# Two attention blocks side by side: first weight rows for six heads in one load, second x pair in two, first products at full width

## The chip, the cores and the metric

The kernel runs on one core of a Trainium2 chip. The metric is the time of one execution in microseconds of device time. A run also has a span, from the first to the last instruction of the core; here the time is about 1.8 us longer than the span. The profile lists instructions by engine: PE (matrix products; PEld are its weight loads, which overlap the products: 213.6 us of them beside 335.2 us of products in a span of 341.2 us), DVE (vector), ACT (scalar), POOL, and SP, which here issues most DMA loads.

## The reference

Two independent blocks, A and B, do the same work on different data, and their outputs stand side by side in the last dimension. Cut to what matters:

```python
# x [16, 32, 1024], k_cache/v_cache [16, 4, 512, 128], wq [1024, 4096], wo [4096, 1024], bf16
def block(x, k_cache, v_cache, wq, wo):
    q = (x @ wq).reshape(16, 32, 32, 128).transpose(0, 2, 1, 3)
    k, v = (jnp.repeat(t, 8, axis=1) for t in (k_cache, v_cache))   # 8 query heads per KV head
    p = softmax(einsum("bhqd,bhkd->bhqk", q, k) * 128 ** -0.5)
    o = einsum("bhqk,bhkd->bhqd", p, v)
    return o.transpose(0, 2, 1, 3).reshape(16, 32, 4096) @ wo
# result: concatenate([block(A), block(B)], axis=-1)
```

The change touches only the first microseconds of block A: `x @ wq` for the first eight heads.

## The kernel before

x has 512 tokens (TT = 4 tiles of 128) and 1024 columns (DC = 8 chunks of 128). The product for one head and one chunk takes 128 rows of wq as weights and 128 rows of x transposed (xT) as the moving operand, 512 tokens wide. The first four chunks of x are loaded plainly and transposed by PE into PSUM; DVE copies chunks 0 and 2 into SBUF, ACT chunks 1 and 3. The first eight heads are computed chunk by chunk as data arrives (NF = 6 heads first, then the other two). The loads, in order of issue:

```python
load_x(0, TT // 2, TT, nc.scalar)        # x chunks 0-1, second token half, issued by ACT
load_x(0, 0, TT // 2)                    # x chunks 0-1, first token half; this and the rest by SP
load_w0(0, 1, 0, NF // 2)                # wq chunk 0, heads 0-2  (96 KB)
load_w0(0, 1, NF // 2, NF)               # wq chunk 0, heads 3-5  (96 KB)
load_w0(1, 2, 0, NF)                     # wq chunk 1, heads 0-5  (192 KB)
load_x(2, 0, TT)                         # x chunks 2-3           (256 KB)
load_w0(2, 3, 0, NF)                     # wq chunk 2
load_w0(3, 4, 0, NF)                     # wq chunk 3
# ... (heads 6-7, chunks 4-7, the k and v caches)
```

The work of PE at the start, where `transpose_x` is four or two PE transposes and a copy, and `first_heads(heads, chunks, t0, t1)` is one product per head and chunk over the given token tiles:

```python
warm_up(22)                                              # dummy products of 128 columns
for k, ts in enumerate(((0, TT // 2), (TT // 2, TT))):   # token halves
    transpose_x(0, *ts, nc.vector.tensor_copy)
    transpose_x(1, *ts, nc.scalar.copy, spare[k])
for ts in ((0, TT // 2), (TT // 2, TT)):
    first_heads(range(0, NF // 2), (0,), *ts)            # 3 heads, half width, twice
first_heads(range(NF // 2, NF), (0,))                    # 3 heads, full width
first_heads(range(0, NF - 2), (1,))
transpose_x(2, 0, TT, nc.vector.tensor_copy)
transpose_x(3, 0, TT, nc.scalar.copy)
# ... the rest of the first eight heads, then a stream of products for the other heads (L301),
#     scores (L357), values (L425) and the output projection (L320), to the end
```

## Time and profile before

| | before |
|---|---|
| time, median of 3 runs (range) | 343.14 us (342.83 to 343.26) |
| span of the profiled run | 341.2 us |
| PE busy | 335.2 us, 98% |
| first product of chunk 0 starts | 4.17 us |
| first product of the stream (second group of heads) starts | 18.91 us |

The profile's page gives busy time by engine, and the chain of work that ended last, followed back from the last instruction:

```profile
PE 335.2 (98%) x2082; PEld 213.6 (63%) x2121; DVE 265.5 (78%) x336; ACT 185.9 (54%) x209; POOL 46.7 (14%) x206
...
PE 98%; issue 1%; ACT 0%; ACTq 0%
```

PE alone bounds the kernel. The timeline of the start of before follows. Its columns: start in us, length in us, engine, line, operation, output and input, shapes, and how many instructions are merged in the row; in brackets the idle time of the engine before it and what ended it. A merged row names only the first shape: the 13 products of the row at 4.17 are six of half width (256 columns) and seven of full width.

```profile
2.92 0.53 PE L516 MATMUL q_ps<-const-bfloat16-1.0 128*128 128x128 bf16 x3
3.28 1.09 PE L524 MATMUL xT_ps<-ident,x_sb 128*128 128x128 bf16 x8
3.71 0.29 DVE L528 COPY xT<-xT_ps 128x256 bf16<-128x256 bf16 x1 [2.75 <-PE xT_ps L524]
3.92 0.86 ACT L528 COPY xT<-xT_ps 128x256 bf16<-128x256 bf16 x2 [1.32 <-PE xT_ps L524]
4.17 2.79 PE L534 MATMUL q_ps<-xT,w_sb 128*128 128x256 bf16 x13
4.19 0.29 DVE L528 COPY xT<-xT_ps 128x256 bf16<-128x256 bf16 x1 [0.19 <-PE xT_ps L524]
5.79 0.67 PEld L534 LDWEIGHTS <-w_sb 128*128 128x128 bf16 x4 [0.20 <-DMA w_sb<-in_A_wq_dram]
6.79 0.61 PE L524 MATMUL xT_ps<-ident,x_sb 128*128 128x128 bf16 x8
7.45 0.83 PE L534 MATMUL q_ps<-xT,w_sb 128*128 128x512 bf16 x3
```

The products of chunk 0 start at 4.17 us, before DVE has even begun its second copy (4.19 us): the half-width products of the first token half hide that copy. The one weight load that waited (0.20 us at 5.79) cost nothing, because a product was still running (starts at 5.71 and 5.93 us, 0.216 us apart like those after them).

One thing this view doesn't show directly. The start times of single products in the trace tell how fast PE runs: until 5.10 us products of 256 columns start 213 ns apart, after it 110 ns. The array's clock doubles there. Transposes of 128 columns agree: those before 4.17 us start 107 ns apart except around their waits, like the warm-up products, and those from 6.79 us on 56 ns.

### The profile page before, as it was taken

The numbers are of one execution on the slowest core, as the hardware profiler recorded it, in microseconds if no ns is written. First come the engines' busy times: TensorE is split into PE (matmuls) and PEld (weight loads), VectorE is DVE, ScalarE is ACT, GpSimd is POOL, SyncE is SP. The second block draws the span as 40 slices with busy tenths as digits, with TensorE's granted clock in tenths as the row PEclk, the third lists the DMA queues.
The fourth block names the chain that finished last, engine by engine and source line by source line (L and its number), as shares of the span: only waits on it lengthen the run. The fifth ranks groups of instructions, "written<-read, shape, count | busy, mean of one in ns | idle before, by whom it ended". The sixth has DMA issues, their size and how long they took to land.

```text
span 341.2 us, 5454 instructions
## 1 busy us (share of the span) xinstructions
PE 335.2 (98%) x2082; PEld 213.6 (63%) x2121; DVE 265.5 (78%) x336; ACT 185.9 (54%) x209; POOL 46.7 (14%) x206
## 2 busy tenths in 40 slices
PE   8999999999999999999999999999999999999996
PEld 6455666666666666666666666666666666666555
DVE  1046988888988898888888988879888888889540
ACT  3058666666667667666645545555555555555110
POOL 0001110011111111110012221222122101111100
PEclk9999999999999999999999999999999999999999
DMA  7999999999996987899999955998449997430001
GB/s 211 287 190 273 285 249 202 233 242 268 291 248 154 232 242 219 210 314 299 308 306 258 250 125 144 334 268 242 118 103 296 356 187 176 104 97 16 18 18 33
DMA packets 128094, 71.70 MB, mean 210 GB/s; under 512 B 75840, under 2 KB 127296, under 8 KB 128064
## 3 DMA queue, kind: packets, MB, share of 16 engines
q1 hardware_dynamic: 127264, 70.07, 84.1%
q0 software_dynamic: 384, 1.05, 0.9%
q8 instruction: 17, 0.28, 0.3%
q10 hardware_dynamic: 416, 0.20, 0.2%
q14 instruction: 13, 0.11, 0.1%
HBM read 50.86 MB, written 2.10 MB: 155 GB/s over the span
## 4 chain that ended last, share of the span: by engine, by line
PE 98%; issue 1%; ACT 0%; ACTq 0%
PE f_ps L320 32%; PE q_ps L301 28%; PE ob L425 17%; PE s_ps L357 16%; PE q_ps L534 4%; PE q_ps L516 1%; PE xT_ps L524 0%; ACT o_sb L329 0%; ACTq L329 0%
## 5 line engine op out<-in xcount | busy, mean ns | idle before, releaser
L365 ACT ACTIVATE p_sb<-s_ps,shift 128x1024 bf16<-128x1024 f32 x128 | 142.7, 1115 | 97.5 <-PE s_ps L357 88.1
L376 DVE TRANSPOSE_TENSOR_REDUCE parts<-p_sb 128x32 f32<-128x1024 bf16 x128 | 158.7, 1240 | 21.0 <-ACT p_sb L365 19.3
L320 PE MATMUL f_ps<-wo_sb,oT 128*128 128x512 bf16 (+1 forms) x525 | 128.2, 366 | 0.6
L301 PE MATMUL q_ps<-xT,wq_sb 128*128 128x512 bf16 x430 | 113.2, 379 | 0.5
L425 PE MATMUL ob<-p_sb,v_sb 128*128 128x256 bf16 x512 | 76.8, 273 | 0.8
L357 PE MATMUL s_ps<-qT,kT 128*128 128x256 bf16 x512 | 76.8, 273 | 0.0
L320 PEld LDWEIGHTS <-oT 128*128 128x128 bf16 x544 | 53.2, 98 | 35.3
L357 PEld LDWEIGHTS <-kT 128*128 128x128 bf16 x512 | 56.9, 113 | 28.3
L301 PEld LDWEIGHTS <-wq_sb 128*128 128x128 bf16 x448 | 43.8, 98 | 32.2
L425 PEld LDWEIGHTS <-v_sb 128*128 128x128 bf16 x512 | 50.1, 98 | 20.0
L447 DVE TENSOR_TENSOR oT<-r,ob 128x512 bf16<-128x512 f32 x64 | 43.9, 686 | 19.9 <-PE ob L425 19.4
L411 DVE STREAM_TRANSPOSE r<-rall 128x512 f32<-128x512 f32 x64 | 44.2, 691 | 1.1
L309 ACT CAST qT<-q_ps 128x512 bf16<-128x512 f32 x56 | 32.7, 583 | 16.5 <-PE q_ps L301 16.5
L394 POOL COPY half<-cs 64x32 f32<-64x32 f32 x32 | 6.5, 204 | 231.8 <-DVE cs L384 231.8
L329 ACT CAST o_sb<-f_ps 128x512 bf16<-128x512 f32 (+1 forms) x17 | 9.5, 559 | 23.6 <-PE f_ps L320 23.6
L534 PE MATMUL q_ps<-xT,w_sb 128*128 128x512 bf16 (+1 forms) x65 | 14.4, 379 | 0.1
L384 DVE TENSOR_REDUCE cs<-parts 128x32 f32<-128x128 f32 x32 | 12.1, 377 | 1.1
L406 DVE RECIPROCAL rall<-sums 128x32 f32<-128x32 f32 x32 | 10.2, 319 | 3.3 <-POOL sums L403 3.3
L534 PEld LDWEIGHTS <-w_sb 128*128 128x128 bf16 x67 | 6.8, 102 | 7.0 <-DMA w_sb<-in_A_wq_dram 0.2
L560 DVE CAST qT<-q_ps 128x512 bf16<-128x512 f32 x4 | 2.5, 684 | 10.2 <-PE q_ps L534 10.2
L331 POOL DMA_DIRECT2D out_dram<-o_sb x8 | 4.6, 574 | 29.3 <-ACT o_sb L329 29.3
L395 POOL TENSOR_TENSOR half<-half,cs 64x32 f32<-64x32 f32 x32 | 7.8, 243 | 2.6
(25 smaller groups left out, 44.7 us busy)
## 6 DMA issues: line engine op xcount, KB each, us to landing
v_sb<-in_A_v_cache_dram SPq DMA_DIRECT2D x16, 512.0 KB, 5.7
wq_sb<-in_B_wq_dram SPq DMA_DIRECT2D x8, 1024.0 KB, 5.7
wo_sb<-in_A_wo_dram SPq DMA_DIRECT2D x8, 1024.0 KB, 7.4
v_sb<-in_B_v_cache_dram SPq DMA_DIRECT2D x16, 512.0 KB, 4.7
wo_sb<-in_B_wo_dram SPq DMA_DIRECT2D x8, 1024.0 KB, 8.1
wq_sb<-in_A_wq_dram SPq DMA_DIRECT2D x5, 1024.0 KB, 5.8
wq_sb<-in_A_wq_dram SPq DMA_DIRECT2D x2, 512.0 KB, 6.7
kT<-in_A_k_cache_dram SPq DMA_TRANSPOSE x64, 4.4
```

What stands on the lines that cost most here:

```text
L301: nc.tensor.matmul(ps[:], lhsT=w[:, dc, (h % 4) * DH:(h % 4 + 1) * DH], rhs=xT[pr][:, dc, :], start=(dc == 0), stop=(dc == DC - 1),)
L309: nc.scalar.copy(out=qT[pr, g][:, :, hl, :], in_=ps[:].rearrange("p (b s) -> p b s", s=SQ),)
L320: nc.tensor.matmul(ps[:, 0:width], lhsT=oT[pr, tt][:, h, :], rhs=wo_tiles[pr, nh, h // REP][:, h % REP, off:off + width], start=(h == 0), ...
L357: nc.tensor.matmul(s_ps[:, c, :], lhsT=kT[:, i % GRP, c, :], rhs=qT[pr, g][:, b, :, :].rearrange("p h s -> p (h s)"), start=True, stop=True,)
L365: nc.scalar.activation(out=p_sb[:], in_=s_ps[:], func=ACTF.Exp, bias=shift[:], scale=SCALE)
L376: nc.vector.tensor_reduce(out=parts[k][:, q, :, :].rearrange("p c h -> p (c h)"), in_=st[i]["p"][:].rearrange("p c (h s) -> p (c h) s", s=SQ),
L384: nc.vector.tensor_reduce(out=cs[:], in_=parts.pop(k)[:].rearrange("p q c h -> p q h c"), axis=AX.X, op=ALU.add,)
L406: nc.vector.reciprocal(out=rall[:, k, :], in_=quad.pop(k)[:])
L411: nc.vector.transpose(out=r[:].rearrange("p n s -> p (n s)"), in_=rall[:, k, o * 2 * REP:(o + 1) * 2 * REP] .unsqueeze(2).to_broadcast([P, ...
L425: nc.tensor.matmul(ob[j][:, q, :], lhsT=v_sb[:, i % GRP, c, :], rhs=st[i]["p"][:, c, :], start=(c == 0), stop=(c == KC - 1),)
L447: nc.vector.tensor_tensor(out=out, in0=rcp.pop(j)[:].rearrange("p (q h) s -> p q h s", h=REP), in1=ob.pop(j)[:].rearrange("p q (h s) -> p ...
L534: nc.tensor.matmul(first_q[h][:, ts], lhsT=w0[dc // HC][:, dc % HC, h * DH:(h + 1) * DH], rhs=xT[0][:, dc, ts], start=(dc == 0 and t0 == 0 ...
```

## The change

The intent: SP needs about 0.47 us for each issue (in before, its first eight issues, of 96 to 256 KB, start 0.47 to 0.55 us apart), so merging the two loads of wq chunk 0 should bring chunks 0 and 1 in earlier; the free slot is used to split the load of x chunks 2-3. With chunk 0 there for all six heads, its products are done at full width, in six instead of nine instructions.

```diff
             load_x(0, 0, TT // 2)
-            load_w0(0, 1, 0, NF // 2)
-            load_w0(0, 1, NF // 2, NF)
+            load_w0(0, 1, 0, NF)
             load_w0(1, 2, 0, NF)
-            load_x(2, 0, TT)
+            load_x(2, 0, TT // 2)
+            load_x(2, TT // 2, TT)
             load_w0(2, 3, 0, NF)
...
-            for ts in ((0, TT // 2), (TT // 2, TT)):
-                first_heads(range(0, NF // 2), (0,), *ts)
-            first_heads(range(NF // 2, NF), (0,))
+            first_heads(range(NF), (0,))
             first_heads(range(0, NF - 2), (1,))
```

## The prediction

> **What bounds the kernel.** The page's first part has PE busy 335.2 of 341.2 us (98%), its chain that ended last is 98% PE, and the view of waits for PE shows one wait, 0.9 us before the first instruction. A delay of PE at the start is passed on one for one.
>
> **The start, from the timeline.** 22 warm-up matmuls run from 0.93 us at about 107 ns each. The two x halves land at 3.23 and 3.72 us; the 16 transposes end at about 4.17 us. Six half-width products follow (three heads, two token halves), then full-width ones. Until about 5.06 us 256 columns take 213 ns, after that 110 ns: the array's clock doubles.[...]
>
> **What the change was meant to gain.** Landings in the trace: w rows of chunk 0 for heads 0-2 at 3.92, heads 3-5 at 5.03, chunk 1 at 5.75, x chunks 2-3 at 6.55, chunk 2 at 7.06, chunk 3 at 7.77 us. SP needs about 0.47 us per issue whatever its size, so merging two 96 KB loads frees one slot: I estimate chunk 0 whole at about 4.4 us (4.1 to 4.9), chunk 1 at about 5.3 (it is issued 0.47 us earlier). The split x load takes that slot again: from chunk 2 on nothing moves. But none of these loads holds PE up before: the one weight-load wait (0.2 us, chunk 1) is hidden behind the running matmul (starts at 5.710 and 5.925, the normal 216 ns apart), and x chunks 2-3 come just as the array needs them. Earlier loads gain about 0.
>
> **What it costs.** A full-width first product needs both token halves of xT chunk 0. DVE's second copy runs 4.19 to 4.48 us, so the first product can start at about 4.53 instead of 4.17: PE idles about 0.37 us, in place of the half-width products that hid that copy. The idle time is at half clock, so if the doubling stays at 5.06 us it costs 0.37/2 = 0.18 us. If chunk 0 lands at 4.9 it is about 0.4 us.[...]
>
> **Sum:** +0.2 us: 343.35 us, range 342.9 to 344.1. Faster by over 2%: 0.005; within 2%: 0.99; slower by over 2%: 0.005.
>
> **What would show it.** (1) In the timeline, first product of chunk 0 at 4.5 to 4.6 us instead of 4.17, PE idle before it, ended by DVE's copy; if a weight load ends it, the merged load is what binds. (2) Products before 5.06 us at 427 ns for 512 columns, after at 216. (3) Landings: chunk 0 whole between the old 3.92 and 5.03, chunk 1 earlier by about 0.5 us, later ones within 0.2 us. (4) The stream's first product (second group of heads) starts about 0.2 us later than before and the gap stays constant to the last instruction.
>
> **What would make it wrong.** The idle 0.4 us could postpone the clock's doubling[...]. Chunk 0's single load could be held by the slow early reads (packets of up to 0.57 us seen near 4 us). Or x pieces in two loads land later than the one did, and the transposes of chunks 2-3, which had no slack (needed at 6.57, landed at 6.55), wait for them.

The sum is the +0.2 us (343.35 us), 0.37/2 = 0.18 us for the idle time, rounded up, and about 0 for the loads.

## The result, and the profile after

| | before | after |
|---|---|---|
| time, median of 6 runs (range) | 343.2 us (342.83 to 343.48) | 343.29 us (343.18 to 343.73) |
| span of the profiled run | 341.2 us | 341.3 us |
| first product of chunk 0 | 4.17 us | 4.47 us |
| clock doubles (from product start times) | 5.10 us | 4.65 us |
| first product of the stream | 18.91 us | 18.98 us |

The ratio is 1.0005, with a 95% interval of 0.9992 to 1.0018: the same. A ratio in this document is the mean time of one kernel's fast runs over that of the other's of the same rounds, so not quite the ratio of the medians quoted.

The page of after has the same balance, but a step of DVE now stands in the chain. These are the same two lines and the line by source line under them:

```profile
PE 337.1 (99%) x2118; PEld 213.2 (62%) x2118; DVE 265.5 (78%) x336; ACT 185.8 (54%) x209; POOL 46.6 (14%) x206
...
PE 99%; ACT 0%; issue 0%; DVE 0%; ACTq 0%
PE f_ps L320 32%; PE q_ps L301 28%; PE s_ps L357 16%; PE ob L425 16%; PE q_ps L534 4%; PE q_ps L516 1%; PE xT_ps L524 0%; ACT o_sb L329 0%; DVE xT L528 0%; ACTq L329 0%
```

(More recorded PE instructions than before, although the program has three fewer products: some product records are missing from each trace, more of them in that of before.) The timeline of the start of after:

```profile
3.24 1.06 PE L524 MATMUL xT_ps<-ident,x_sb 128*128 128x128 bf16 x8
3.70 0.72 DVE L528 COPY xT<-xT_ps 128x256 bf16<-128x256 bf16 x2 [2.74 <-PE xT_ps L524]
3.91 0.80 ACT L528 COPY xT<-xT_ps 128x256 bf16<-128x256 bf16 x2 [1.32 <-PE xT_ps L524]
4.33 0.25 PEld L534 LDWEIGHTS <-w_sb 128*128 128x128 bf16 x2 [0.29 <-DMA w_sb<-in_A_wq_dram]
4.47 2.38 PE L534 MATMUL q_ps<-xT,w_sb 128*128 128x512 bf16 x10 [0.17 <-DVE xT L528]
6.69 0.61 PE L524 MATMUL xT_ps<-ident,x_sb 128*128 128x128 bf16 x8
7.14 1.21 PE L534 MATMUL q_ps<-xT,w_sb 128*128 128x512 bf16 x4
7.74 0.33 PEld L534 LDWEIGHTS <-w_sb 128*128 128x128 bf16 x3 [0.50 <-DMA w_sb<-in_A_wq_dram]
```

Three things are to be seen. The first product starts at 4.47 us and DVE's copy ended the wait. The bracket says 0.17 us because the profile lets a product end late; from start times, the last transpose's slot ends at 4.10 us, and the array idles 0.33 us (a product that had to wait is recorded late, and the next one follows so much sooner: in before, after the two waits for x, the next transpose starts 82 instead of 107 ns later; here it is some 0.05 us, an estimate from the starts at 4.47 and 4.75 us and the doubling at 4.65). The merged load of chunk 0 landed at 4.28 us, before the copy was done, so it wasn't what bound. And there is a new wait: the weights of chunk 2 came only at 7.70 us (semaphore events; 7.06 in before), and the products at 7.36 and 7.75 us stand 0.39 us apart instead of 0.216.

Two losses, 0.33 us of idle time at half clock and 0.17 us at full clock, and yet the stream starts only 0.07 us later. The clock doubled 0.45 us earlier in this run. Was that the change, or the run? This is what the experiments are for.

### The profile page after: what moved, and what is told of

The parts are those of the page before. It is cut to its first block, busy times and chain, and to the rows that moved or that the text cites. A ratio compares the mean times of both kernels' runs of the same rounds, so it can differ in the third digit from the quotient of the medians.

```text
span 341.3 us, 5487 instructions
## 1 busy us (share of the span) xinstructions
PE 337.1 (99%) x2118; PEld 213.2 (62%) x2118; DVE 265.5 (78%) x336; ACT 185.8 (54%) x209; POOL 46.6 (14%) x206
## 4 chain that ended last, share of the span: by engine, by line
PE 99%; ACT 0%; issue 0%; DVE 0%; ACTq 0%
PE f_ps L320 32%; PE q_ps L301 28%; PE s_ps L357 16%; PE ob L425 16%; PE q_ps L534 4%; PE q_ps L516 1%; PE xT_ps L524 0%; ACT o_sb L329 0%; DVE xT L528 0%; ACTq L329 0%
## 5 line engine op out<-in xcount | busy, mean ns | idle before, releaser
L320 PE MATMUL f_ps<-wo_sb,oT 128*128 128x512 bf16 (+1 forms) x544 | 132.3, 367 | 0.0
L301 PE MATMUL q_ps<-xT,wq_sb 128*128 128x512 bf16 x448 | 116.9, 379 | 0.0
L534 PE MATMUL q_ps<-xT,w_sb 128*128 128x512 bf16 x64 | 14.4, 380 | 0.2 <-DVE xT L528 0.2
L534 PEld LDWEIGHTS <-w_sb 128*128 128x128 bf16 x64 | 6.1, 98 | 7.7 <-DMA w_sb<-in_A_wq_dram 0.8
```

The costliest lines, as they stand in the source:

```text
L301: nc.tensor.matmul(ps[:], lhsT=w[:, dc, (h % 4) * DH:(h % 4 + 1) * DH], rhs=xT[pr][:, dc, :], start=(dc == 0), stop=(dc == DC - 1),)
L320: nc.tensor.matmul(ps[:, 0:width], lhsT=oT[pr, tt][:, h, :], rhs=wo_tiles[pr, nh, h // REP][:, h % REP, off:off + width], start=(h == 0), ...
L534: nc.tensor.matmul(first_q[h][:, ts], lhsT=w0[dc // HC][:, dc % HC, h * DH:(h + 1) * DH], rhs=xT[0][:, dc, ts], start=(dc == 0 and t0 == 0 ...
```

## The experiments

Twelve kernels were run in three groups, all correct. The theory after the first look: the loads gain nothing because none was on the path; the full-width products cost the idle time before the second copy, halved by the slow clock; the start reaches the end one for one; and the time at which the clock doubles is a matter of the run. Rivals: the loads gain and the products give it back; delays at the start are absorbed later; the new load order delays chunk 2.

### The change in two halves, and both kernels again

before_again and after_again are unedited. The two halves:

```diff
# loads_only: before with
-            load_w0(0, 1, 0, NF // 2)
-            load_w0(0, 1, NF // 2, NF)
+            load_w0(0, 1, 0, NF)
             load_w0(1, 2, 0, NF)
-            load_x(2, 0, TT)
+            load_x(2, 0, TT // 2)
+            load_x(2, TT // 2, TT)
# products_only: before with
-            for ts in ((0, TT // 2), (TT // 2, TT)):
-                first_heads(range(0, NF // 2), (0,), *ts)
-            first_heads(range(NF // 2, NF), (0,))
+            first_heads(range(NF), (0,))
```

> The kernel before, unchanged, as a measure of noise. Both theories: ratio 1.000, interval within about 0.1%. Trace: first product of chunk 0 at 4.17 us, as in the first profile, no idle time over 0.15 us in the array between 3.3 and 4.2 us. If the time at which the array's clock doubles (5.1 us in the first profile of before, 4.6 in that of after) is a matter of each run and not of the kernel, it differs here from 5.1 us by some tenths, and the start of the second group of heads moves by half of that.

> Merged first load and split x pair, half-width products kept. My theory (the loads were not on the array's path): ratio 1.000 (0.999 to 1.001); first product at 4.1 to 4.2 us, no idle time before it; chunk 0 whole at about 4.3 us, chunk 1 at about 5.4. Rival (earlier loads do gain, and the full-width products give it back): faster by 0.3 us or more, 0.999 or less, and the second group of heads starts earlier than in before by that much beyond half of the shift of the clock's doubling. Second rival (the new load order delays chunks 2 and 3): chunk 2 lands after 7.4 us again and the array waits for it by 0.1 to 0.3 us around 7.5 us; in before it landed at 7.06.

> Full-width first products, old loads. My theory: first product at about 4.5 us after 0.3 to 0.4 us of idle array, ended by DVE's copy; all of the change's cost is here: +0.1 to +0.2 us, ratio 1.0003 to 1.0006, hard to tell from 1 in the times, but the second group of heads starts 0.1 to 0.2 us later than in before once half of the shift of the clock's doubling is taken off. Chunk 2 lands at about 7.1 us as before, no wait for it. Heads 3 to 5 of chunk 0 land at about 5.0 us, needed at about 5.3: no or a small wait. Rival (nothing at the start reaches the end): start of the second group of heads unchanged.

> The changed kernel, unchanged, for a second trace and more times. My theory: ratio 1.0003 to 1.0008; first product at 4.4 to 4.6 us, ended by DVE's copy. If the late landing of chunk 2 (7.70 us, 0.17 us of waiting in the first profile of after) comes with the load order, it is seen again: landing at 7.4 us or later; if it was chance, it lands at 6.9 to 7.2 us and the array doesn't wait.

Measured, five runs each against nine of before (median 343.54 us): before_again 1.0004 (0.999 to 1.0017), loads_only 1.0009 (0.9996 to 1.0023), products_only 1.0002 (0.9989 to 1.0016), after_again 0.9999 (0.9985 to 1.0012). No time tells any of them from before, nor before from itself. The spans of before_again's runs lie at 341.4, 341.5, 341.6, 342.2 and 342.2 us: the same program varies by more than the change could be worth. Its profiled run, one of the 342.2, shows where. PE's rows of the timeline:

```profile
3.35 1.03 PE L524 MATMUL xT_ps<-ident,x_sb 128*128 128x128 bf16 x8
4.18 3.75 PE L534 MATMUL q_ps<-xT,w_sb 128*128 128x256 bf16 x13
```

The same 13 products from the same start took 3.75 us, against 2.79 in the first profile of before. The clock doubled at 7.06 us here.

This gives a sum that can be checked in each trace. A microsecond before the doubling does half the work (256 columns take 213 ns before it and 110 after it in before), so the doubling at time F costs F/2; an idle time before F costs half of itself; a wait after it costs all. With one constant, 16.30 us, fitted to these traces, the start of the stream should be 16.30 + F/2 + (idle before F)/2 + (waits after F). F, idle times and waits are read from the start times of single products, but for F of loads_only, explained below the table; "stream to end" is the span less the stream's start. The four lower rows are from experiments further down.

| trace | F | idle before F | waits after F | sum | stream starts | stream to end |
|---|---|---|---|---|---|---|
| before | 5.10 | 0.07 | 0.02 | 18.91 | 18.91 | 322.31 |
| before_again | 7.06 | 0.09 | 0.02 | 19.90 | 19.88 | 322.31 |
| after | 4.65 | 0.33 | 0.18 | 18.97 | 18.98 | 322.30 |
| after_again | 6.63 | 0.38 | 0.02 | 19.83 | 19.82 | 322.31 |
| products_only | 5.37 | 0.33 | 0.02 | 19.17 | 19.17 | 322.31 |
| loads_only | 4.19 | 0.13 | 0.37 | 18.83 | 18.85 | 322.31 |
| w_merged | 5.29 | 0.15 | 0.49 | 19.51 | 19.51 | 322.37 |
| x_split | 4.77 | 0.25 | 1.03 | 19.84 | 19.85 | 322.73 |
| dose_before | 6.52 | 0.06 | 0.02 | 19.61 | 19.61 | 322.31 |
| dose_after | 5.04 | 0.70 | 0.02 | 19.19 | 19.19 | 322.31 |

The sum holds to 0.02 us in all ten. The trace files also keep records of the granted clock, which no view prints. Their start agrees with F to 0.02 us in the other nine (5.095 us in before, 4.635 in after). In loads_only the clock doubled as the last transpose ended and the array then stood idle, so product starts can't date the doubling; the record says 4.19 us, and the second product starts 119 ns after the first, close to the 109 ns of the doubled clock and far from the 213 before it. The rows of the timeline of loads_only, then of products_only, that start the products of chunk 0:

```profile
4.34 0.98 PEld L534 LDWEIGHTS <-w_sb 128*128 128x128 bf16 x9 [0.17 <-DMA w_sb<-in_A_wq_dram]
4.34 2.34 PE L534 MATMUL q_ps<-xT,w_sb 128*128 128x256 bf16 x13
```

```profile
3.70 0.72 DVE L528 COPY xT<-xT_ps 128x256 bf16<-128x256 bf16 x2 [2.74 <-PE xT_ps L524]
4.47 2.74 PE L534 MATMUL q_ps<-xT,w_sb 128*128 128x512 bf16 x10 [0.17 <-DVE xT L528]
```

What follows:

- The rest of the kernel takes 322.3 us whatever happens at the start; delays are not absorbed. That rival falls. (In x_split the last output's write ended 0.4 us later than elsewhere, after the last product.)
- loads_only doesn't gain. It waited 0.13 us for x before the doubling, and after it about 0.14 us for the merged chunk 0 (landed at 4.30 us, where heads 0-2 alone had landed at 3.92 in before) and 0.22 us for chunk 2. The rival that loads gain what the products lose falls.
- products_only and both traces of after have 0.33 to 0.38 us of idle time before the doubling, the two of before 0.07 and 0.09. Halved, the difference is about 0.14 us: the cost of the full-width products.
- F moves from run to run by far more than all that.

### A gate that takes the clock out

To make a difference of 0.2 us visible in times, the real start is held back until the clock has doubled in every run, and all early loads have landed. DVE does a chain of dummy transposes, PE's transposes need a copy of the identity made after it, and PE is kept busy meanwhile:

```diff
# gated_before, gated_after: before and after with (rall is not in use yet)
+            nc.vector.memset(flat_rall[:, 0:512], 0.0)
+            for _ in range(12):
+                nc.vector.transpose(out=flat_rall[:, 512:1024], in_=flat_rall[:, 0:512])
+            ident_late = const.tile([P, P], BF16, name="ident_late")
+            nc.vector.tensor_copy(out=ident_late[:], in_=ident[:])
...
-                        ps[:, tt * P:(tt + 1) * P], x_sb[:, tt, d * P:(d + 1) * P], ident[:]
+                        ps[:, tt * P:(tt + 1) * P], x_sb[:, tt, d * P:(d + 1) * P], ident_late[:]
...
-            warm_up(22)
+            warm_up(80)
```

> The kernel before, with its first transposes held back by a chain of fixed length on the vector engine (12 transposes of 0.69 us, estimate: until about 9.5 us) and 80 instead of 22 warm-up products, so that the array's clock has doubled and all first loads have landed before the real work starts. My theory (the spread between runs comes from when the clock doubles, and the start reaches the end one for one): the spans of the five runs lie within 0.2 us of each other, where those of before spread over 1.0 us; second group of heads at about 24.4 us, and from there to the end 322.3 us as in all six traces so far, so a span of about 346.7 us. Rival (the spread comes from elsewhere, from the 320 us that follow): spans spread over 0.6 to 1.0 us as before. Rival (delays of the start are absorbed later): less than 322.2 us from the second group to the end.

> The changed kernel with the same gate and warm-up. Loads play no part, the clock neither. My theory: the full-width first products wait for the second copy while the half-width ones hide it; at full clock that costs the whole wait, 0.25 to 0.35 us, so the spans are 0.2 to 0.35 us longer than those of gated_before, clear of a spread below 0.2 us, ratio of the two 1.0006 to 1.001. Rival (the width of the first products costs nothing): same span within 0.05 us.

This failed as a measurement, and was instructive. The spans were 347.8 us once and 349.4 to 349.5 four times (gated_before), 348.1 once and 349.5 to 349.7 four times (gated_after): two groups 1.4 to 1.7 us apart, not a spread below 0.2 us. The chain lasted until 10.6 us, PE had run out of dummies at 7.5, and the clock fell back. In the timeline of gated_before, a run of the longer kind, full-width products after the fallback:

```profile
10.61 0.61 PE L530 MATMUL xT_ps<-ident_late,x_sb 128*128 128x128 bf16 x8 [2.97 <-DVE ident_late L240]
...
12.35 2.77 PE L540 MATMUL q_ps<-xT,w_sb 128*128 128x512 bf16 x6 [0.22 <-issue]
```

The six products start 427 ns apart; at full clock, as in the row at 7.45 us of before, they start 216 ns apart. From start times the clock doubled at 5.09 us, fell back at about 11.9 and doubled again at 15.33. These lie about 2 x 3.41 and 3 x 3.41 us after the first; 3.41 us at half clock cost up to 3.41/2 = 1.7 us, about the distance of the two groups. The clock records of all fourteen traces show the same step: in gated_before full clock is granted for 6.827 us and then half for 3.413 us, which are two steps and one; elsewhere full clock lasts 334.506, 337.919 or 341.333 us, which are 98, 99 or 100 times 3.413 us.

The second gate has 9 transposes in the chain and 74 warm-up products; otherwise it is the same edit.

> The first gate was too long: the array sat idle for 3.0 us and its clock fell back to half in most runs (spans 347.8 or 349.5). Here the chain is 9 transposes of 0.74 us and 74 warm-up products, so the array idles at most 1.6 us. My theory: no fallback; real work starts at about 8.45 us in every run, spans within 0.2 us of each other at about 345.7 us, second group of heads at about 23.4 us, then 322.3 us. Rival (the spread between runs comes from elsewhere): spans spread over 0.8 us or more, as in before (341.2 to 342.2).

> The changed kernel with the same gate. My theory: spans within 0.2 us of each other, 0.2 to 0.35 us longer than those of gate2_before (the two unthrottled runs of the first gate stood at 347.8 and 348.1): the wait for the second copy at full clock. Rival (no cost of the full-width products): same within 0.05 us.

Now four of four spans are 345.6 us for gate2_before and four of four 345.8 us for gate2_after. The times are 347.39, 347.39, 347.40 and 347.50 us against 347.60, 347.71, 347.72 and 347.72: means 347.42 and 347.69, 0.27 us apart, with no overlap. So the run-to-run spread of the plain kernels does come from the start: with the clock out of the way, it falls from 1.0 us to less than 0.1 in the spans. And the cost of the full-width products is there. The start of gate2_before, then of gate2_after, timeline:

```profile
8.37 0.61 PE L530 MATMUL xT_ps<-ident_late,x_sb 128*128 128x128 bf16 x8 [1.60 <-DVE ident_late L240]
8.68 0.52 DVE L534 COPY xT<-xT_ps 128x256 bf16<-128x256 bf16 x2 [0.36 <-PE xT_ps L530]
9.03 0.81 PE L540 MATMUL q_ps<-xT,w_sb 128*128 128x256 bf16 x6
```

```profile
8.37 0.61 PE L530 MATMUL xT_ps<-ident_late,x_sb 128*128 128x128 bf16 x8 [0.53 <-DVE ident_late L240]
8.68 0.52 DVE L534 COPY xT<-xT_ps 128x256 bf16<-128x256 bf16 x2 [0.36 <-PE xT_ps L530]
9.25 0.81 PE L540 MATMUL q_ps<-xT,w_sb 128*128 128x512 bf16 x2 [0.27 <-DVE xT L534]
```

The transposes and copies agree to 0.01 us; the first product starts at 9.03 or at 9.25 us, after one copy or after two. The stream starts at 23.31 and 23.53 us, 0.22 later, and the profiled spans differ by 0.22 us (345.62 and 345.84). The rival that the width costs nothing falls.

### Why chunk 2 comes late

```diff
# w_merged: before with
-            load_w0(0, 1, 0, NF // 2)
-            load_w0(0, 1, NF // 2, NF)
+            load_w0(0, 1, 0, NF)
# x_split: before with
-            load_x(2, 0, TT)
+            load_x(2, 0, TT // 2)
+            load_x(2, TT // 2, TT)
```

> Only the merging of the two loads of chunk 0; x chunks 2-3 in one load, half-width products. In the three traces with the new load order chunk 2 landed at 7.57 to 7.98 us, in the three with the old one at 7.01 to 7.26. If the merging makes that (every later load is issued one slot, 0.47 us, earlier here): chunk 2 at 7.4 us or later although it is issued at about 2.7 us. If it is the split x pair: 7.1 us or earlier, about 6.6 to 7.0. Chunk 0 whole at about 4.3 us, in either case a short idle time of the array before the first product when x lands early.

> Only the split of x chunks 2-3 into two loads; chunk 0's rows in two loads as before. All loads from chunk 2 on are issued one slot, 0.47 us, later than in before. If the split of x makes chunk 2 late: 7.9 us or later (the 0.6 us seen, and 0.47). If only the slot counts: about 7.4 to 7.6 us. If the merging made it: also 7.4 to 7.6. The array then waits for chunk 2 when the clock doubles early (before about 5 us), and does not when it doubles after about 6 us.

In w_merged chunk 2 landed at 7.99 us, though issued a slot earlier than in before: as the merging theory expected. In x_split, at 7.48 us: as the slot alone explains. But in w_merged x chunks 2-3 were also late (7.33 us; PE waited 0.46 us for them), and in x_split PE waited 0.67 us for chunk 3 (9.87 us), 0.20 for chunk 1 and 0.11 for heads 3-5 of chunk 0. So there are late arrivals (tails) in the landings, and by the time of landing alone one look can't tell them from an effect. Each of these loads leaves 16 arrivals (semaphore events) in the trace, and the weight loads wait for the last: the one that waited for chunk 2 in after starts at 7.74 us, 0.04 us after the last arrival at 7.70, though the median of the 16 is 6.30 us, earlier than the 6.63 in before.

Over all twelve traces with one of the two full load orders, chunk 2 landed at 7.01 to 7.79 us with the old one (six traces, mean 7.28) and at 7.43 to 8.11 with the new one (six traces, mean 7.72). The means differ by 0.44 us, and the ranges overlap. That it comes later with the new order is likely. The arrivals say which half of the change goes with it. The lag of the last of chunk 2's 16 arrivals behind their median is 0.26 to 0.57 us in the seven traces that load chunk 0 in two pieces, x_split among them (0.40), and 0.76 to 1.45 us in the seven that load it in one, w_merged among them (1.15). The two groups don't overlap, so the tail goes with the merging and not with the split of x. The lag was chosen as a measure after the fact, and each half stands alone in one trace only; what in the merged load delays the last arrivals is left open. It costs time only where PE is early: the wait of about 0.2 us is there in after (F at 4.65) and loads_only (4.19), and not in after_again (6.63), where chunk 2 landed later still, at 7.98 us, nor in dose_after (5.04).

### A larger dose of the same idle time

The second copy of x chunk 0 is held up by other work on DVE:

```diff
# dose_before, dose_after: before and after with
             for k, ts in enumerate(((0, TT // 2), (TT // 2, TT))):
+                if k == 1:
+                    nc.vector.transpose(out=flat_rall[:, 512:1024], in_=flat_rall[:, 0:512])
                 transpose_x(0, *ts, nc.vector.tensor_copy)
```

> The kernel before with 0.74 us of other work on the vector engine between its two copies of x chunk 0, so that the second copy ends at about 5.05 instead of 4.48 us. The half-width products of the first token half run meanwhile; idle time about 0.3 us at half clock. My theory: +0.1 to +0.2 us, ratio about 1.0005; clock doubles between 4.3 and 7.8 us as in the ten traces so far.

> The changed kernel with the same 0.74 us. The full-width products can't start before about 5.1 us: the array idles about 0.9 us in place of 0.33. My theory as it stands, idle time alone: +0.45 us over before, ratio 1.0013. My second theory[...] the doubling comes one window later, and the runs are 1.5 to 2.1 us longer, with the trace's doubling after 7.8 us in most cases. Rival (the time of the doubling doesn't depend on what the array does): doubling between 4.3 and 7.8 us, ratio 1.0013.

(The window is the step of 3.41 us seen in gated_before.)

Measured: dose_before 0.9995 (0.9982 to 1.0008), dose_after 1.0006 (0.9985 to 1.0027). The dose was smaller than planned. The copy was recorded as starting at 4.53 instead of 4.19 us, a shift of 0.34 us and not 0.57, because it overlaps the end of the transpose (recorded from 3.91 to 4.61 us in dose_before). From start times, dose_after idled 0.70 us before its first product at 4.84, where after idled 0.33; dose_before idled 0.06 us. The half-width products hid all but these 0.06 us of the dose, and the full-width ones hid nothing.

The second theory, that the idle time puts off the doubling, came out in one run of six at best, and not in most. The six spans of dose_after are 341.4, 341.4, 341.5, 341.6, 341.9 and 343.6 us. By the sum above, the last needs a doubling at about 9.2 us: 2 x (343.6 - 322.31 - 16.30 - 0.35 - 0.02). In no other run of an ungated kernel did the span exceed 342.6 us. That run has no trace, so this remains an inference. What decides the doubling is not shown either. The profiled run doubled at 5.04 us, and in the 3.41 us before that PE was busy for 79% (3.41 less 0.70 us). In before_again it had been busy for 77% of the 3.41 us before 7.06 - 3.41 = 3.65 us (PE starts at 0.93 us), and the clock didn't double then. (These shares count PE's transposes as busy.) Two traces so close to each other don't tell one cause from another.

## Why the prediction was right or wrong

The time was right: 343.35 us predicted, 343.29 measured, inside 342.9 to 344.1, within 2%. But the agreement to 0.06 us is luck, since runs of the same kernel before lie up to 1.3 us apart (342.83 to 344.09).

- **PE bounds the kernel, and a delay at the start is passed on one for one: right.** The stream takes 322.3 us to the end in nearly every trace, gated or not.
- **Earlier loads gain about 0: right.** Chunk 0 whole landed at 4.28 us (estimate 4.4). loads_only shows no gain.
- **First product at 4.5 to 4.6 us, ended by DVE's copy: right**, at 4.47 us.
- **"it costs 0.37/2 = 0.18 us": right in mechanism, somewhat too large.** The idle time is 0.33 to 0.38 us, but before too idles 0.07 to 0.09 us at that point, waiting for x; the difference halved is 0.14 us. At full clock, the second gate measured 0.22 us in the trace and 0.27 us in the times.
- **"from chunk 2 on nothing moves": wrong.** Chunk 2 landed at 7.70 instead of 7.06 us and cost 0.17 us in the profiled run. Chunk 1 came only 0.28 us earlier there (5.47 instead of 5.75), not 0.5, and in after_again it came at 6.16. The late arrivals of chunk 2 go with the merged load in all fourteen traces; by what path is not settled.
- **"if the doubling stays at 5.06 us": this is the step that failed.** The prediction took one run's value for the kernel's. F lay between 4.19 and 7.06 us in the ten traces without a gate. It alone moves the time by F/2, so by up to 1.4 us between these traces, about ten times what the change costs. For the same reason the stream started 0.07 us later in the profiled pair and not 0.2: F came 0.45 us earlier (-0.23), the idle time cost +0.13 and the wait for chunk 2 +0.16.
- **The idle time could put off the doubling: not seen for the changed kernel itself** (eleven runs, spans up to 342.1 us), and perhaps once when the idle time was doubled (dose_after, the run with a span of 343.6 us).

Over all runs of the plain kernels, after has a mean of 343.41 us (11 runs) and before one of 343.49 (40 runs), with standard deviations of 0.27 and 0.32. But all runs of after are from the first measurement and the first group, and the last group ran on another chip; the 20 runs of before from the same two sets have a mean of 343.39. The times alone can't place a cost of 0.14 us. No experiment pointed to a version that beats both: before idles only about 0.1 us between its first transpose and the stream, so at this place there is little left to win but the doubling itself, which no kernel here controls.

## What to carry to other kernels

Before loads are sped up, look whether the engine ever waits for them: here none was on the path, and narrower first products that hid a copy were worth more than three saved instructions. Where a change is worth less than the spread of the runs, find what makes the spread and gate it out, or write the start as a sum (clock, idle times, waits) and check it in several traces; one pair of profiles would have shown 0.07 us here and explained nothing. An idle microsecond at half clock cost half here (the sum with F/2 and half of the idle time held to 0.02 us in ten traces), and a load counted when the last of its 16 arrivals was in (chunk 2 in after: 7.70 us, median 6.30), so the median arrival tells little.
